# fp32 score products on both row halves, and grouped state and value products, in a gated linear attention with a feed-forward block

## The chip, the cores and the metric

The kernel runs on one core of a Trainium2 chip. The metric is the device time of one execution in microseconds; lower is better. A core has five engines with their own queues: PE (matrix products into PSUM), DVE (vectors), ACT (scalar functions), POOL (a second vector engine without access to PSUM) and SP (which issues the DMAs here). PSUM has eight banks of 512 fp32 values a row.

## The reference

Four batches, eight heads, 768 tokens, 48 channels a head. Each head keeps a 48 x 48 state that decays by alpha and takes up k times v; its rows go through a feed-forward layer of 384 -> 2048 -> 384.

```
for t in range(S):
    state = alpha[:, :, t, :, None] * state + np.einsum('bhd,bhe->bhde', k[:, :, t], v[:, :, t])
    y[:, :, t] = np.einsum('bhd,bhde->bhe', q[:, :, t], state)
...
h = x @ w_in
g = np.maximum(0.01 * h, h)
return (g @ w_out).astype(np.float32)
```

The weights come as 64-bit floats; the kernel turns each into a high and a low part of type fp32r (fp32 stored with fewer bits of mantissa, which PE takes in one pass).

## The kernel before

**Units.** The work of attention is cut into 24 units: 6 chunks of 128 tokens by 4 batches, `u = 4 * chunk + batch`. Within a chunk the products of alpha are kept as P (forward scan, L257) and 1/P (backward scan, L262), so that y = mask(scaled k times scaled q) times v, plus state times scaled q. Heads are held in pairs: head 2p in rows 0 to 47 and head 2p+1 in rows 64 to 111 of every tile, four pairs side by side. Three units make one block of 384 rows for the feed-forward part, so there are 8 blocks.

**Steps of a unit** (generator `attention`, L399): `scans`, `scores` for s = 0 and 1, `k_tokens` (k turned back by PE, L339), `scaled_q` and `scaled_k` of the unit after, `outputs` (y), `next_state` (L376, L385, L386). After every third unit `gather` moves rows of x by DMA. From unit 6 on (`SPLIT`), `parts` (L288) splits scaled k and q into high and low fp32r parts: three casts on ACT (L297, L301 twice) and three subtractions on POOL (L298, L302 twice). The two heads of a pair have columns of their own in `qh` and `ql`, zero elsewhere, so one product of 112 rows and 256 columns gives the scores of both; each pair takes three (high x high, high x low, low x high), twelve for a unit (L317), six to a PSUM bank. Each bank is then masked by one DVE product (L327). Units 0 to 5 have plain fp32 products of one head each over 48 rows (L311), and the mask of s = 0 by an ACT copy (L322) and a POOL select (L323).

**y** (`outputs`): for each of four pairs one product with the state (L354, 112 rows, both heads), then the value product of the first head (L356, into PSUM rows 0 to 47) and of the second (L357, into rows 64 to 111). ACT then casts y to its high part (L361) and DVE subtracts for the low one (L362).

**Feed-forward.** `ffn_in` (L437): nine products of 128 x 384 into bank `ph`, for each of 16 slices f; leaky maximum by ACT (L440) and DVE (L441), split by ACT (L443) and DVE (L445). `ffn_out` (L453): nine products into three banks held for the whole block. While block 0 runs, the weights are converted (L178 to L210) on ACT, DVE and POOL.

**Order.** Attention steps are called out between the feed-forward slices (L483 to L513). The framework then orders the instructions of each engine anew, by its own simulation of their times, and may keep more buffers where memory is free. PSUM: two `ph` banks, three of tag "a", three of tag "b". From unit 6 on attention uses the "b" banks in rotation for two score tiles, turned k, y and the state's product.

Of the kernel before, what the change touches and what calls it, by code (L numbers as in the profile page):

```python
# [14 lines left out]
AF = mybir.ActivationFunctionType  # L15
ALU = mybir.AluOpType

# bound on the sums of |P| and |1/P| over a chunk
RANGE = 2.0 ** 40


# [1 line left out]
def gated_linear_attn_ffn(ctx, tc, q, k, v, alpha, w_in, w_out, out):  # L23
# [34 lines left out]
    PITCH = RUN + GAP  # L58
    EARLY = 2 * UPB
    CATCH = 9  # L60
    SPLIT = EARLY
    LAG = 2
    SL = 8 * UPB

# [3 lines left out]
        return ps_x.tile([P, 512], F32, name=tag or att_bank[0])  # L68

    def pieces(name, dtype, *shapes):  # L70
        """One tile, cut into parts of these shapes a partition."""
        sizes = [math.prod(shape) for shape in shapes]
        whole = cst.tile([P, sum(sizes)], dtype, name=name)
        parts = []
        for n, shape in enumerate(shapes):
            part = whole[:, sum(sizes[:n]):sum(sizes[:n + 1])]
            axes = "abc"[:len(shape)]
            if len(shape) > 1:
                part = part.rearrange(f"p ({' '.join(axes)}) -> p {' '.join(axes)}", **dict(zip(axes, shape)))
            parts.append(part)  # L80
        return parts
# [14 lines left out]
    def load(u, i):  # L96
        if u >= NU:
            return
        tb, b = units[u]
        ts = slice(tb * C, (tb + 1) * C)  # L100
        t, src = loaded(u, i), (alpha, q, k)[i]
        if u < EARLY:
            n = H if u or i else H // 2
            for h in range(0, H, n):
                nc.sync.dma_start(
                    by_token(t)[:, h:h + n, 0:D], src[b, h:h + n, ts, :].rearrange("h t d -> t h d")
                )
            return
        # 32 partitions a head and half of its channels: runs of four tokens, shifted by 32 channels for the second
        for a in range(4):  # L110
            off = 32 * (a % 2)
            nc.sync.dma_start(
                t[32 * a:32 * (a + 1), :].rearrange("j (p r) -> j p r", p=NP)[:, :, 0:RUN - off],
                src[b, a // 2::2, ts, :].rearrange("p (j t) d -> j p (t d)", t=T4)[:, :, off:],
            )
# [29 lines left out]
        nc.gpsimd.memset(state[b], 0.0)  # L145


    # row r of group g of x is this row of w_in
    runs = [(0, D, 0, 2 * D), (D, GAP, 6 * D, GAP), (HB, D, D, 2 * D), (BR, GAP, 7 * D, GAP)]

    # the weights come as jobs: w_in and w_out for one f after the other
    jobs = {}

    def load_weights(j):
# [16 lines left out]
    def convert_1(j):  # L171
        if not f64:
            return
        raw, = jobs[j]
        words = raw.rearrange("p g (f w) -> p g f w", w=2)
        top, low = words[:, :, :, 1], words[:, :, :, 0]
        rest = cvp.tile([P, NG, P], F32, name="rest", bufs=NREST)
        nc.scalar.activation(rest, low.bitcast(U32), AF.Copy, scale=2.0 ** -52)  # L178
        # read as a float32, the upper word has the exponent in steps of eight: 2**-112 moves float64's bias to float32's
        nc.scalar.mul(top.bitcast(F32), top.bitcast(F32), 2.0 ** -112)  # L180
        jobs[j] = top, rest

# [37 lines left out]
        return bank().rearrange("r (p n) -> r p n", p=NP)  # L220

    def transposed(u, i, name, **kw):
        """The channels of a unit by rows: on TensorE into PSUM, later on VectorE into SBUF."""
        src = loaded(u, i)
        if u < EARLY:
            ps = banks4()
# [8 lines left out]
        )  # L235
        return t

    # two blocks of x; the last two heads of either come into the group between them first
    xs = {}

    live, masked = {}, {}
    q_split = [cst.tile([P, NP, 2, C], F32R, name=n) for n in ("qh", "ql")]

    # the reversed products start again from a reciprocal every STEP tokens
    STEP = 16
    nc.gpsimd.memset(seed, 0.0)

# [37 lines left out]
        nc.vector.tensor_tensor(ks, kT, rc, ALU.mult)  # L285
        live[u] = [pe, qs, ks]

    def parts(u):  # L288
        """The high and low parts of scaled k, and of scaled q with the heads of a pair in columns of their own."""
        if u == SPLIT:  # L290
            for q in q_split:
                nc.gpsimd.memset(q.bitcast(F32), 0.0)
        pe, qs, ks = live[u][:3]
        qh, ql = q_split
        kh = atp.tile([P, NP, C], F32R, name="kh", bufs=1)
        kl = atp.tile([P, NP, C], F32R, name="kl", bufs=1)
        nc.scalar.copy(kh, ks)  # L297
        nc.gpsimd.tensor_tensor(kl, ks, kh.bitcast(F32), ALU.subtract)  # L298
        for s, lo in ((0, 0), (1, HB)):
            r = slice(lo, lo + D)  # L300
            nc.scalar.copy(qh[r, :, s, :], qs[r])  # L301
            nc.gpsimd.tensor_tensor(ql[r, :, s, :], qs[r], qh[r, :, s, :].bitcast(F32), ALU.subtract)  # L302
        live[u] += [kh, kl]

    def scores(u, s):
        pe, qs, ks = live[u][:3]
        ss = banks4()
        if u < SPLIT:
            lo = s * HB
            for p in range(NP):  # L310
                nc.tensor.matmul(ss[:, p, :], ks[lo:lo + D, p, :], qs[lo:lo + D, p, :], start=True, stop=True)  # L311
        else:
            kh, kl = live[u][3:5]
            qh, ql = q_split
            for p in (2 * s, 2 * s + 1):
                for n, (kt, qt) in enumerate(((kh, qh), (kh, ql), (kl, qh))):
                    nc.tensor.matmul(  # L317
                        ss[:, 2 * (p % 2):2 * (p % 2) + 2, :], kt[0:BR, p, :], qt[0:BR, p, :, :], start=n == 0, stop=n == 2
                    )
        sm = atp.tile([P, NP, C], F32, name="sm", bufs=3)  # L320
        if u < EARLY and s == 0:
            nc.scalar.copy(sm, ss)  # L322
            nc.gpsimd.affine_select(  # L323
                out=sm, in_=sm, compare_op=ALU.is_ge, fill=0.0, base=0, pattern=[[0, NP], [1, C]], channel_multiplier=-1
            )
        else:
            nc.vector.tensor_tensor(sm, ss, mask.unsqueeze(1).broadcast_to([P, NP, C]), ALU.mult)  # L327
        masked.setdefault(u, []).append(sm)

    def masked_scores(u, p, s):  # L330
        a, b = masked[u]
        return (b if s else a)[:, p, :] if u < SPLIT else (b if p > 1 else a)[:, 2 * (p % 2) + s, :]

    def k_tokens(u):
        if units[u][0] < NC - 1:
# [8 lines left out]
    def outputs(u):  # L344
# [3 lines left out]
        V, W = vals_sb[u % NV], state[b]  # L348
        at = NG * (i % 2)
        y = banks4()  # L350
        for p in range(NP):
            r = (p + i % 2) % NP
            if tb:
                nc.tensor.matmul(y[0:BR, r, :], W[0:BR, p, :], qs[0:BR, p, :], start=True, stop=False)  # L354
            m = D if tb else HB
            nc.tensor.matmul(y[0:m, r, :], V[:, 2 * p * D:2 * p * D + m], masked_scores(u, p, 0), start=not tb, stop=True)  # L356
            nc.tensor.matmul(  # L357
                y[HB:BR, r, :], V[:, (2 * p + 1) * D:(2 * p + 2) * D], masked_scores(u, p, 1), start=not tb, stop=True
            )
        xh, xl = (x_sb[0:BR, n, at:at + NP, j * C:(j + 1) * C] for n in (0, 1))  # L360
        nc.scalar.copy(xh, y[0:BR])  # L361
        nc.vector.tensor_tensor(xl, y[0:BR], xh.bitcast(F32), ALU.subtract)  # L362
# [23 lines left out]
            nc.gpsimd.tensor_tensor(W[r, :, r], us[r], pe[r].broadcast_to([D, NP, D]), ALU.mult)  # L386

    def gather(i):
        """The last two heads go to the rows left free beside the others."""
        at = (NG + 1) * (i % 2)  # L390
        xs[i] = [x_sb[:, n, at:at + NG, :] for n in (0, 1)]
        x = x_sb.bitcast(F32)
        for g in range(NG):
            for lo in (0, HB):
                nc.sync.dma_start(x[lo + D:lo + HB, :, at + g, :], x[lo + g * GAP:lo + (g + 1) * GAP, :, NG, :])
# [1 line left out]
    ready = set()  # L397

    def attention(first, last):  # L399
        """The scaled q and k of a unit are made beside the products of the one before."""  # L400
        for u in range(first - 1, last):
            new, old = u + 1 < last, u >= first
            if new:
                scans(u + 1)
                yield
            if old:
                for s in (0, 1):
                    scores(u, s)
                    yield
                k_tokens(u)  # L410
                yield
            if new:
                scaled_q(u + 1)
                yield
                scaled_k(u + 1)
                if u + 1 >= SPLIT:
                    parts(u + 1)
                yield
            if old:
                outputs(u)  # L420
# [49 lines left out]
    while 0 not in ready:  # L470
        next(st)

    # (block, f, weight jobs and slices of attention beside it): the first block goes ahead alone, then with the second
    LEAD = NF - CATCH
    items = [(0, f, 2, SL / (CATCH - 1)) for f in range(CATCH)]
    for n in range(LEAD):
# [6 lines left out]
    for n in range(len(items) + LAG):  # L483
# [15 lines left out]
        for half in range(2):  # L499
            due += slices / 2  # L500
            while emitted < due:
                # what follows the first blocks' attention stays behind the last of the weights on VectorE
                with tc.issue_after(made[0, NF - 2].ins) if held else nullcontext():
                    next(st, None)
                held = max(held - 1, 0)
# [6 lines left out]
                    if i == 0:  # L512
                        att_bank[0], st, held = "b", attention(EARLY, NU), 5  # L513

    # the chunked form holds where no product of alphas in a chunk leaves the range; else step by step
    fine = cst.tile([P, 2 * NU], F32, name="fine")
    nc.vector.tensor_scalar(fine, acc, RANGE, None, ALU.is_lt)
    least = cst.tile([P, 1], F32, name="least")
# [8 lines left out]
    def stepwise(ctx):  # L527
        gp = ctx.enter_context(tc.tile_pool(name="gp", bufs=2))
        gps = ctx.enter_context(tc.tile_pool(name="gps", bufs=1, space=bass.MemoryType.PSUM))
        L, V = [by_token(loads_sb[i][0]) for i in range(3)], vals_sb[0]  # L530
        # the place of head h among x's rows: pieces (first e, number, row)
        place = {h: [(0, D, (h // 2) * HB)] for h in range(2 * NG)}
        for s in (0, 1):
            place[2 * NG + s] = [(g * GAP, GAP, g * HB + D) for g in range(NG)]
# [112 lines left out]
```

## Time and profile before

| | |
|---|---|
| median of 3 runs | 619.03 us (618.51 to 619.93) |
| span of the profiled execution, first to last instruction | 618.7 us |
| granted TensorE clock, mean | 0.959 |
| y products L354, L356, L357 of units 6 to 23, mean busy time of one instruction | 314, 299, 299 ns |
| feed-forward products L437, mean | 346 ns (overlapping; start to start about 173) |

A fp32 product appears as two PE instructions, a fp32r product as one. Matrix products are pipelined, so an instruction's duration is longer than the distance to the next start; the distance is the cost. "PEld" is the load of the stationary operand. A row of the timeline gives start, duration, engine, line, operation, what is written <- what is read, shape, count, and in brackets the idle time before it with what ended it.

### The profile page before, as it was taken

The page shows a single profiled execution, that of the slowest core. Times are in us where ns is not written, and L with a number is a line of the kernel's source. Part 1 is how long each engine was busy: PE and PEld are TensorE (multiplying, and loading weights), DVE is VectorE, ACT ScalarE, POOL GpSimd, SP SyncE. Part 2 cuts the span into 40 slices and gives each one's busy share as a digit, 9 for nine tenths or more (in the row PEclk, how much of TensorE's full clock was granted, in tenths as well). Part 3 has the DMA queues.
Part 4 walks back from the last instruction along what each step waited for, and adds up shares of the span by engine and source line. Part 5 has one row for each costly group of instructions (what it writes and reads, how often), then busy time and mean ns, then how long its engine had stood idle before and what let it go on. Part 6 is the DMA issues. An engine that isn't in the chain of part 4 may idle for free.

```text
span 618.7 us, 10006 instructions
## 1 busy us (share of the span) xinstructions
PE 575.9 (93%) x3634; PEld 526.4 (85%) x3634; DVE 444.9 (72%) x777; ACT 269.0 (43%) x577; POOL 205.6 (33%) x216
## 2 busy tenths in 40 slices
PE   6856998779999879999999999999999999999995
PEld 4745977779888758998898889998898989999995
DVE  5999999998999979836766678576856655333331
ACT  4656556443554425433443454243533433224332
POOL 4597588773334433400321234032220231000000
PEclk9787897989999869999999999999999999999999
DMA  9996745311533445202421244022301120011001
GB/s 167 203 190 151 179 110 149 108 51 32 149 78 77 101 105 152 58 1 55 122 48 38 55 109 110 19 65 56 100 23 37 38 70 1 1 20 40 1 1 42
DMA packets 90087, 48.11 MB, mean 78 GB/s; under 512 B 49584, under 2 KB 87984, under 8 KB 90032
## 3 DMA queue, kind: packets, MB, share of 16 engines
q1 hardware_dynamic: 90032, 47.41, 34.0%
q8 instruction: 30, 0.49, 0.3%
q14 instruction: 25, 0.20, 0.1%
HBM read 40.30 MB, written 4.72 MB: 73 GB/s over the span
## 4 chain that ended last, share of the span: by engine, by line
PE 63%; DVE 16%; issue 3%; DMA 2%; ACT 1%; SPq 1%; POOL 0%; DVEq 0%; ACTq 0%
PE a L453 25%; PE ph L437 25%; PE b L354 4%; PE b L356 3%; PE b L317 3%; DVE gl L445 2%; DVE pc L257 2%; DVE bits L199 2%; PE b L376 2%; DVE t L441 2%; DVE bits L198 2%; DVE large L210 1%; DMA small<-in_k_dram 1%; DVE pw L200 1%; DVE e L232 1%
## 5 line engine op out<-in xcount | busy, mean ns | idle before, releaser
L437 PE MATMUL ph<-large 128*128 128x384 f32 x1152 | 233.7, 346 | 7.7 <-DVE t L441 4.9
L437 PEld LDWEIGHTS ph<-large 128*128 128x128 f32 x1152 | 206.0, 193 | 13.5 <-DVE t L441 7.4
L453 PE MATMUL a<-large,gh 128*128 128x384 f32 x672 | 172.3, 343 | 0.0
L441 DVE TENSOR_TENSOR t<-ph,t 128x384 f32<-128x384 f32 x128 | 69.9, 550 | 86.2 <-ACT t L440 86.1
L453 PEld LDWEIGHTS a<-large,gh 128*128 128x128 f32 x672 | 120.2, 190 | 1.7 <-issue 0.7
L440 ACT ACTIVATE t<-ph 128x384 f32<-128x384 f32 x128 | 62.1, 489 | 117.8 <-PE ph L437 113.4
L445 DVE TENSOR_TENSOR gl<-t,gh 128x384 fp32r<-128x384 f32 x128 | 84.7, 663 | 38.1 <-ACT gh L443 37.9
L453 PE MATMUL a<-large,gl 128*128 128x384 f32 x336 | 110.5, 340 | 0.8 <-DVE gl L445 0.8
L443 ACT CAST gh<-t 128x384 fp32r<-128x384 f32 x128 | 65.4, 512 | 92.2 <-DVE t L441 91.6
L386 POOL TENSOR_TENSOR small<-us,pe 48x192 f32<-48x192 f32 x32 | 20.8, 650 | 155.1 <-DVE us L385 145.2
L453 PEld LDWEIGHTS a<-large,gl 128*128 128x128 f32 x336 | 62.8, 188 | 1.6 <-DVE gl L445 1.1
L302 POOL TENSOR_TENSOR ql<-qs,qh 48x512 fp32r<-48x512 f32 x36 | 50.0, 1388 | 8.7 <-ACT qh L301 7.3
L202 POOL TENSOR_TENSOR rest<-pw,rest 128x384 f32<-128x384 f32 x32 | 35.7, 1115 | 33.1 <-DVE pw L200 29.3
L298 POOL TENSOR_TENSOR kl<-ks,kh 128x512 fp32r<-128x512 f32 x18 | 25.2, 1400 | 60.7 <-ACT kh L297 41.0
L203 POOL TENSOR_TENSOR bits<-bits,large 128x384 f32<-128x384 f32 x32 | 38.1, 1189 | 0.7 <-ACT large L201 0.7
L268 ACT ACTIVATE e<-pc 128x512 f32<-128x512 f32 x24 | 15.2, 632 | 50.8 <-DVE rc L262 42.8
L356 PE MATMUL b<-sm,small 128*48 128x128 f32 x144 | 31.2, 299 | 3.6 <-DVE sm L327 3.6
L354 PE MATMUL b<-qs,small 112*112 112x128 f32 x144 | 33.3, 314 | 0.0
L357 PE MATMUL b<-sm,small 128*48 128x128 f32 x144 | 31.2, 299 | 0.0
L257 DVE TENSOR_TENSOR_SCAN pc<-e,small 128x128 f32<-128x128 f32 x72 | 30.1, 477 | 0.6
L354 PEld LDWEIGHTS b<-qs,small 112*112 112x112 f32 x144 | 21.1, 179 | 10.6 <-issue 10.5
L232 DVE STREAM_TRANSPOSE qs<-small 128x512 f32<-128x512 f32 x18 | 19.8, 1097 | 10.6 <-PE b L354 9.1
(93 smaller groups left out, 812.4 us busy)
## 6 DMA issues: line engine op xcount, KB each, us to landing
raw<-in_moe_w_out_dram SPq DMA_DIRECT2D x16, 384.0 KB, 3.4
small<-in_v_dram SPq DMA_DIRECT2D x24, 192.0 KB, 3.3
raw<-in_moe_w_in_dram SPq DMA_DIRECT2D x32, 144.0 KB, 3.2
out_dram<-t SPq DMA_DIRECT2D x24, 192.0 KB, 2.3
small<-in_alpha_dram SPq DMA_DIRECT2D x38, 96.0 KB, 2.2
small<-in_k_dram SPq DMA_DIRECT2D x36, 96.0 KB, 2.2
small<-in_q_dram SPq DMA_DIRECT2D x36, 96.0 KB, 2.2
small<-in_alpha_dram SPq DMA_DIRECT2D x36, 80.0 KB, 2.4
```

Of the source, the lines that this page charges most:

```text
L202: nc.gpsimd.tensor_tensor(rest, pw.bitcast(F32), rest, ALU.mult)
L203: nc.gpsimd.tensor_tensor(val, val, hi.bitcast(F32), ALU.subtract)
L257: nc.vector.tensor_tensor_scan(pc[:, p, :], aT[:, p, :], ones.broadcast_to([P, C]), 1.0, ALU.mult, ALU.mult)
L302: nc.gpsimd.tensor_tensor(ql[r, :, s, :], qs[r], qh[r, :, s, :].bitcast(F32), ALU.subtract)
L354: nc.tensor.matmul(y[0:BR, r, :], W[0:BR, p, :], qs[0:BR, p, :], start=True, stop=False)
L356: nc.tensor.matmul(y[0:m, r, :], V[:, 2 * p * D:2 * p * D + m], masked_scores(u, p, 0), start=not tb, stop=True)
L437: nc.tensor.matmul(ph, wt[:, g, fs], xt[:, g, :], start=n == 0, stop=n == 3 * NG - 1)
L440: nc.scalar.mul(t, ph, 0.01)
L441: nc.vector.tensor_tensor(t, ph, t, ALU.max)
L443: nc.scalar.copy(gh, t)
L445: made[i, f] = nc.vector.tensor_tensor(gl, t, gh.bitcast(F32), ALU.subtract)
L453: nc.tensor.matmul(po[j], gt[:, js], wt[:, f, :], start=f == 0 and n == 0, stop=f == NF - 1 and n == 2)
```

## The change

Units from 6 on lose `parts`, with its tiles `qh`, `ql`, `kh` and `kl`, and get the form of the early units: eight fp32 products of 48 rows and 128 columns, pair after pair, each pair's two heads one after the other, into two banks at once. The mask becomes a step of its own for all units: s = 0 by ACT and POOL, s = 1 by DVE. In y, the four state products come first and the eight value products behind them; only the first product of the bank has the start flag.

```
-    def parts(u):
...
-        nc.scalar.copy(kh, ks)
-        nc.gpsimd.tensor_tensor(kl, ks, kh.bitcast(F32), ALU.subtract)
...
-            nc.scalar.copy(qh[r, :, s, :], qs[r])
-            nc.gpsimd.tensor_tensor(ql[r, :, s, :], qs[r], qh[r, :, s, :].bitcast(F32), ALU.subtract)
...
+    def scores(u):
+
+        pe, qs, ks = live[u]
+        ss = [banks4(), banks4()]
+        for p in range(NP):
+            for s, lo in ((0, 0), (1, HB)):
+                nc.tensor.matmul(ss[s][:, p, :], ks[lo:lo + D, p, :], qs[lo:lo + D, p, :], start=True, stop=True)
+        live[u].append(ss)
+
+    def mask_scores(u):
+        ss = live[u].pop()
+        sm = [atp.tile([P, NP, C], F32, name="sm", bufs=3) for _ in (0, 1)]
+        nc.scalar.copy(sm[0], ss[0])
+        nc.gpsimd.affine_select(
+            out=sm[0], in_=sm[0], compare_op=ALU.is_ge, fill=0.0, base=0, pattern=[[0, NP], [1, C]], channel_multiplier=-1
+        )
+        nc.vector.tensor_tensor(sm[1], ss[1], mask.unsqueeze(1).broadcast_to([P, NP, C]), ALU.mult)
+        masked[u] = sm
...
+        if tb:
+            for p, r in enumerate(rot):
+                nc.tensor.matmul(
+                    y[0:BR, r, :], W[0:BR, p, :], qs[0:BR, p, :], start=p == 0, stop=False, skip_group_check=True
+                )
+        for p, r in enumerate(rot):
+            for s, lo, m in ((0, 0, D if tb else HB), (1, HB, D)):
+                c = (2 * p + s) * D
+                nc.tensor.matmul(
+                    y[lo:lo + m, r, :], V[:, c:c + m], masked[u][s][:, p, :],
+                    start=not tb and p == 0, stop=p == NP - 1, skip_group_check=True,
+                )
```

The order of PE's queue for y of unit 12, before (the numbers tell tiles of one name apart; `b_3231` is y, `sm_3087` and `sm_3113` the two masked score tiles, `ph` the feed-forward bank):

```order
L354 MATMUL b_3231<-qs_2912,small_73 112x128
L356 MATMUL b_3231<-sm_3087,small_73 48x128
L357 MATMUL b_3231<-sm_3087,small_73 48x128
L354 MATMUL b_3231<-qs_2912,small_73 112x128
L356 MATMUL b_3231<-sm_3087,small_73 48x128
L357 MATMUL b_3231<-sm_3087,small_73 48x128
L354 MATMUL b_3231<-qs_2912,small_73 112x128
```

The same place in the changed kernel, where L326 is the state product and L332 the value product, and `b_3142` is y:

```order
L310 MATMUL b_3069<-small_73,ks_2875 128x112 x4
L326 MATMUL b_3142<-qs_2842,small_73 112x128 x4
L332 MATMUL b_3142<-sm_3029,small_73 48x128
L332 MATMUL b_3142<-sm_3030,small_73 48x128
L332 MATMUL b_3142<-sm_3029,small_73 48x128
L332 MATMUL b_3142<-sm_3030,small_73 48x128
```

The four state products now stand together, and value products from the two masked tiles alternate behind them, eight in all. (From here on L413 is the old L437, L429 the old L453, L292 the score product, L353 the old L376, L302 the DVE mask, L339 the old L362.)

Scores on PE in the changed kernel, for unit 12 (`b_3002` is the bank of s = 0, `b_3003` that of s = 1; four more rows alternate in the same way):

```order
L429 MATMUL a_2263<-large_74,gl_2873 128x384
L292 MATMUL b_3002<-qs_2842,ks_2875 128x128
L292 MATMUL b_3003<-qs_2842,ks_2875 128x128
L292 MATMUL b_3002<-qs_2842,ks_2875 128x128
L292 MATMUL b_3003<-qs_2842,ks_2875 128x128
```

And for unit 9, with the beginning of its y (`b_2450`); before, the twelve L317 of that unit stood here in two groups of six:

```order
L292 MATMUL b_2310<-qs_2211,ks_2218 128x128 x4
L429 MATMUL a_1256<-large_74,gh_2186 128x384 x2
L429 MATMUL a_1256<-large_74,gl_2188 128x384
L429 MATMUL a_1257<-large_74,gh_2186 128x384 x2
L429 MATMUL a_1257<-large_74,gl_2188 128x384
L429 MATMUL a_1258<-large_74,gh_2186 128x384 x2
L292 MATMUL b_2311<-qs_2211,ks_2218 128x128 x4
L429 MATMUL a_1258<-large_74,gl_2188 128x384
L310 MATMUL b_2377<-small_73,ks_2218 128x112 x4
L326 MATMUL b_2450<-qs_2211,small_73 112x128 x4
L332 MATMUL b_2450<-sm_2337,small_73 48x128
L413 MATMUL ph_2264<-large_74 128x384 x3
```

In unit 12 the two halves alternate; in unit 9, as in unit 7, each half is a group of its own with feed-forward products between, and in unit 10 one group follows the other. In units 13, 16, 19 and 22 feed-forward products stand inside the scores: their eight products come in groups of 2, 5 and 1 in the first three and of 3, 2, 1, 1 and 1 in the last.

More of the change, by code (lines that the diff above doesn't have):

```diff
@@ L60, in gated_linear_attn_ffn @@
     CATCH = 9
-    SPLIT = EARLY
     LAG = 2
@@ L241, in gated_linear_attn_ffn @@
     live, masked = {}, {}
-    q_split = [cst.tile([P, NP, 2, C], F32R, name=n) for n in ("qh", "ql")]
     STEP = 16
@@ L286, in scaled_k @@
         live[u] = [pe, qs, ks]
-    def parts(u):
[L290 to L300, printed above, removed]
-            nc.scalar.copy(qh[r, :, s, :], qs[r])
-            nc.gpsimd.tensor_tensor(ql[r, :, s, :], qs[r], qh[r, :, s, :].bitcast(F32), ALU.subtract)
-        live[u] += [kh, kl]
@@ L305, in scores @@
[L305 to L328, printed above, removed]
@@ L330, in masked_scores @@
-    def masked_scores(u, p, s):
-        a, b = masked[u]
-        return (b if s else a)[:, p, :] if u < SPLIT else (b if p > 1 else a)[:, 2 * (p % 2) + s, :]
+    def scores(u):
[14 more added lines that the diff above has]
+        masked[u] = sm
@@ L350, in outputs @@
         y = banks4()
[L351 to L359, printed above, removed]
+        rot = [(p + i % 2) % NP for p in range(NP)]
+        if tb:
[10 more added lines that the diff above has]
+                )
+        del masked[u]
         xh, xl = (x_sb[0:BR, n, at:at + NP, j * C:(j + 1) * C] for n in (0, 1))
@@ L406, in attention @@
             if old:
-                for s in (0, 1):
-                    scores(u, s)
-                    yield
+                scores(u)
+                yield
+                mask_scores(u)
+                yield
                 k_tokens(u)
@@ L415, in attention @@
                 scaled_k(u + 1)
-                if u + 1 >= SPLIT:
-                    parts(u + 1)
                 yield
```

## The prediction

> **What bounds the kernel now.** I read the busy shares, then the slices, the windows, and last the timeline of single groups.
>
> ```profile
> PE 575.9 (93%) x3634; PEld 526.4 (85%) x3634; DVE 444.9 (72%) x777; ACT 269.0 (43%) x577; POOL 205.6 (33%) x216
> ...
> PE   6856998779999879999999999999999999999995
> ...
> DVE  5999999998999979836766678576856655333331
> ...
> PE 63%; DVE 16%; issue 3%; DMA 2%; ACT 1%; SPq 1%; POOL 0%; DVEq 0%; ACTq 0%
> ```
>
> Two stages. Over the first third DVE stands at 9 and PE does not; from slice 16 on PE is at 9 to the end. The windows put the border near 237 us:
>
> ```profile
> 150.00:176.80 26.80, 25.67 (x149) 24.51 (x148) 26.56 (x50) 13.85 (x31) 6.97 (x8) 1.00 0.47 117
> 176.80:200.00 23.20, 22.20 (x171) 19.17 (x170) 23.01 (x40) 8.90 (x21) 10.17 (x8) 1.00 0.38 86
> 200.00:237.00 37.00, 31.12 (x193) 25.65 (x191) 32.33 (x55) 16.73 (x38) 15.58 (x18) 0.82 0.45 104
> 203.30:206.70 3.40, 3.40 (x15) 3.30 (x16) 3.31 (x10) 0.90 (x2) 1.37 (x3) 0.50 0.87 199
> 220.40:230.60 10.20, 10.17 (x48) 7.29 (x49) 6.92 (x11) 2.03 (x5) 1.59 (x2) 0.50 0.48 110
> 250.80:545.60 294.80, 294.80 (x1900) 273.11 (x1899) 189.65 (x331) 119.04 (x251) 62.72 (x64) 1.00 0.22 52
> ```
>
> (The columns are length, busy PE, PEld, DVE, ACT, POOL, then the granted clock, DMA share and GB/s.) From 250.8 PE never rests and has its full clock, so every PE slot saved there is saved from the end. From 150 to 200 DVE is busy for 49.6 of 50 us. The changed units (numbers 6 to 23, 18 of 24) begin in that stretch. What comes before 150 us keeps its work; only its order is a little different. I cost it at nothing, because DVE has the same instructions there; the order and the buffers that the freed tiles leave room for may move it by 1.5 us either way, an estimate (about one feed-forward group). The DMAs stay the same in number and size.
>
> **The change on PE, slot by slot.** A slot is the time from one start to the next. One unit's products for y, and the feed-forward group behind them:
>
> ```profile
> 365.54 0.38 PE L354 MATMUL b<-qs,small 112*112 112x128 f32 x2
> 365.85 0.31 PE L356 MATMUL b<-sm,small 128*48 128x128 f32 x1
> 365.85 0.31 PE L357 MATMUL b<-sm,small 128*48 128x128 f32 x1
> 366.00 0.27 PE L356 MATMUL b<-sm,small 128*48 128x128 f32 x1
> ...
> 366.20 0.47 PE L354 MATMUL b<-qs,small 112*112 112x128 f32 x2
> ...
> 368.48 1.83 PE L437 MATMUL ph<-large 128*128 128x384 f32 x9
> 370.24 0.56 PE L376 MATMUL b<-small,ktok 128*48 128x48 f32 x8
> ...
> 384.72 1.72 PE L437 MATMUL ph<-large 128*128 128x384 f32 x9
> 386.28 0.52 PE L453 MATMUL a<-large,gh 128*128 128x384 f32 x2
> ```
>
> A fp32 product is two instructions. L356 and L357 start together, as they write different rows of PSUM. y takes 368.48 - 365.54 = 2.94 us. The first state product's second half comes 0.38 - 0.27 = 0.11 behind its first; later ones, behind a value product, need 0.47 - 0.27 = 0.20, and each crossing between the two shapes costs 0.20 where a slot is 0.11. Nine feed-forward products between two groups of small tiles take 1.76, and 1.56 undisturbed: 0.20 for one way in and out. Value products that follow one another show their slot earlier in the program:
>
> ```profile
> 53.43 0.27 PE L357 MATMUL a<-sm,small 128*48 128x128 f32 x1
> 53.44 0.27 PE L356 MATMUL a<-sm,small 128*64 128x128 f32 x1
> 53.54 0.27 PE L357 MATMUL a<-sm,small 128*48 128x128 f32 x1
> ```
>
> A pair every 0.11. New y: 4 state products, 8 x 0.11 = 0.87, plus 0.09 for the crossing; then 16 value instructions in 8 pairs, 0.15 + 6 x 0.11 + 0.20 = 1.00. Sum 1.96, so **0.98 us less a unit**.
>
> Scores, now and in the early units, which have the new form:
>
> ```profile
> 358.98 0.28 PE L317 MATMUL b<-qh,kh 112*128 112x256 f32 x1
> ...
> 360.42 0.26 PE L339 MATMUL b<-small,ks 112*128 112x112 f32 x1
> ...
> 29.57 1.71 PE L311 MATMUL a<-qs,ks 48*128 48x128 f32 x16
> ...
> 85.43 1.16 PE L311 MATMUL a<-qs,ks 48*128 48x128 f32 x8
> 86.52 0.32 PE L339 MATMUL a<-small,ks 112*128 112x112 f32 x1
> ```
>
> Now 12 products in 1.44 us. Four fp32 products of one half of the rows: 86.52 - 85.43 = 1.09. Eight, the halves one after the other, have 1.44 us between first and last start (1.71 - 0.27). In series that would be 15 slots of 0.11 and 0.10 more for the first, 1.78; so three slots were shared by both halves. Halves do run side by side, where the queue brings them together. With the halves alternating, I take 8 products for the time of 4: 1.09, plus 0.20 for going in and out, 1.29: **0.15 less**. Bounds: 1.09 (0.35 less) if the crossing hides, and 16 slots in series, 1.99 + 0.20 (0.75 more).
>
> [...]
>
> The order of the changed program takes some back. From unit 10 on feed-forward products break four units' scores (13, 16, 19, 22) ten extra times. A break costs the 0.20 outside and 0.19 inside a group (1.09 less 8 slots): 10 x 0.39 = 3.9. Five products lose their partner: 5 x 0.22 = 1.1. Unit 10 has its halves one after the other: 0.6. L376, the products for the next state, is broken five times where it was broken nine times: 4 x 0.39 = 1.5 back. Unit 9's rest of y gains 0.7. From unit 9's first value product on: 14 x 1.13 + 0.7 + 1.5 - 3.9 - 1.1 - 0.6 = **12.4 us less**.
>
> **The crowded stretch.** Here PE waits and its clock falls:
>
> ```profile
> 203.18 0.51 PE L317 MATMUL b<-qh,kh 112*128 112x256 f32 x1 [2.28 <-DVE large L362]
> ...
> 220.43 0.45 PE L356 MATMUL b<-sm,small 128*48 128x128 f32 x1 [3.60 <-DVE sm L327]
> ...
> 158.87 2.31 DVE L262 TENSOR_TENSOR_SCAN rc<-e,rc,small 128x511 f32<-128x511 f32 x1
> ...
> 191.53 4.50 DVE L257 TENSOR_TENSOR_SCAN pc<-e,small 128x128 f32<-128x128 f32 x4
> ...
> 216.98 2.68 DVE L257 TENSOR_TENSOR_SCAN pc<-e,small 128x128 f32<-128x128 f32 x4
> ...
> 371.38 1.37 DVE L257 TENSOR_TENSOR_SCAN pc<-e,small 128x128 f32<-128x128 f32 x4
> ...
> 191.08 1.67 POOL L298 TENSOR_TENSOR kl<-ks,kh 128x512 fp32r<-128x512 f32 x1 [2.53 <-ACT kh L297]
> 192.70 2.74 POOL L302 TENSOR_TENSOR ql<-qs,qh 48x512 fp32r<-48x512 f32 x2
> ```
>
> Unit 9's mask, late on DVE, releases PE at 220.43. DVE's four scans take 4.50 us while POOL splits k and q, and 1.37 when it does not: 3.1 us lost at once. From 157 to 219 eight DVE groups are stretched so, all beside those POOL splits, from a split at 157.88 (0.5 lost) and the scan at 158.87 to the scans at 216.98; against their clean selves they lose 8.9 us. The change takes the three POOL splits away and one of a unit's two DVE masks:
>
> ```profile
> L327 DVE TENSOR_TENSOR sm<-b,small 128x512 f32<-128x512 f32 x36 | 24.3, 682 | 3.7 <-PE b L317 3.3
> ...
> L323 POOL TENSOR_SCALAR_AFFINE_SELECT sm<-sm 128x512 f32<-128x512 f32 x6 | 4.8, 794 | 1.4 <-ACT sm L322 1.3
> ...
> L322 ACT COPY sm<-a 128x512 f32<-128x512 f32 x6 | 3.5, 581 | 1.0 <-PE a L311 0.6
> ```
>
> A DVE mask takes a slot of 0.6 there. Masks of units 6 to 8: 3 x 0.6 = 1.8 off; but unit 9's only DVE mask now stands behind a reciprocal, a copy and a backward scan, 1.7 more. So DVE gains what POOL gives back: 8.9, less what the new POOL mask takes, between nothing and 4 x 0.8. The mask ends at 211 to 215 in place of 220.3. PE gets there at about 212: its old arrival, 220.43 - 3.60 = 216.8, less the wait of 2.28 and half of the 3.4 us at half clock, less 3 x 1.13, plus 2.4 because units 7 and 9 have their halves in separate groups. Its first value products need only the POOL half, so I take 212.5, nearer to PE's end: **7.9 us less**, bounds 5 and 9.
>
> **The clock.** After the waits of 2.28 and 3.60 us come spells at half clock; the second (220.4 to 230.6, 0.50 in the window) costs 5.1 us of PE work. A wait under 2 us may leave none. I take half: **2.5 less**, bounds 0 and 5.1. [...]
>
> ACT loses three casts a unit and gains the copy; POOL loses three subtracts and gains the mask; neither bounds. In the long stage 27 feed-forward products (4.7 us) or more stand between a unit's scores and its value products; copy and mask need 0.58 + 0.79 us, and that is the cover: without it, 1.4 us a unit.
>
> Sum: 7.9 + 12.4 + 2.5 = 22.8; 618.7 - 22.8 = 595.9 of span. The runs' median stands 0.3 above the span: **596.2 us**.
>
> **Rivals.**
> - The stretch clears wholly: PE is never late and the clock holds. 0.5 more at unit 9 and 2.6 of clock: 593.1. For it: POOL falls nearly idle there. Against: DVE is full from 150 to 200 now, and loses only a mask and the stretching.
> - The stretch stays: DVE is no faster, unit 9 comes at 220.4, the spell too. Only 12.4: 606.6. For it: DVE has the same chain but one mask. Against: 4.50 beside 1.37.
> - The halves do not share slots: 0.90 a unit, on 14 units 12.6 less the 1.7 already charged, 10.9: 607.1. For it: in the 16-instruction row only three slots were shared. Against: the column pairs alternate in the same way and share every slot.
> - Slower. The halves fill two of the three PSUM banks of the attention at once, so all scores, and not the second half alone, wait for the bank of the former y, which DVE reads last (L362). At 203.18 that wait was 2.28. The gain is 22.8 / 18 = 1.27 us a unit, so it decides from 1.3 us at each unit; at 2.28 it gives 596.2 + 41.0 = 637.2. Against: in the long stage the split follows y quickly (0.8 us after y's last slot), and 18 feed-forward products stand between y and the next scores.
>
> ```profile
> 398.69 0.61 PE L453 MATMUL a<-large,gh 128*128 128x384 f32 x2
> ...
> 399.45 0.68 DVE L362 TENSOR_TENSOR large<-b,large 112x512 fp32r<-112x512 f32 x1
> ```
>
> **Chances.** Forecast 0.62 (593 to 602); wholly clear 0.12; stays 0.12; no sharing 0.08; slower 0.04; the last 0.02 unforeseen. The range takes the first three whole and reaches to the fourth: 588 to 606.8, 588 is a clear stretch with the scores' crossing hidden too (18 x 0.2 = 3.6) and 1.5 from the reordered start. By these cases faster is 0.94, slower 0.04, no change 0.02; 0.2% is about what a measurement of this kernel can tell from none.
>
> **What would show it.** y at about 2.0 us from state product to next group; scores at 1.1 where they alternate, with halves 0.01 apart; unit 9's first value product at 211 to 214; DVE's four scans back at 1.4 and POOL without subtracts; PE from 250 on still without rest. A y that stays at 2.9, scores near 2 us, or a release by the mask's copy, by POOL or by DVE's split at every unit would prove me wrong.

## The result, and the profile after

| | before | after |
|---|---|---|
| median | 619.02 us (4 runs, 618.51 to 619.93) | 596.09 us (4 runs, 594.61 to 597.35) |
| ratio | | 0.9623, 95% interval 0.9599 to 0.9646 |
| profiled execution | span 618.7 us | 594.61 us, span 592.9 us |

The profiled execution is the fastest of the four, so the two profiles lie 25.8 us apart and the medians 22.9. Of the changed kernel's lines, L299 is the POOL mask, L255 and L260 are DVE's scans, and L362 is DVE's part of the next state.

The busy shares and PE's slices after the change:

```profile
PE 550.6 (93%) x3706; PEld 516.1 (87%) x3706; DVE 414.2 (70%) x759; ACT 249.5 (42%) x541; POOL 138.7 (23%) x178
...
PE   5865989699999999999999999999999999999995
```

PE has 72 more instructions and is busy 25 us less. The windows of the stretches that the prediction used, with the same columns:

```profile
150.00:176.80 26.80, 25.34 (x157) 24.48 (x157) 25.93 (x52) 12.56 (x31) 1.15 (x4) 1.00 0.46 117
176.80:200.00 23.20, 21.17 (x178) 19.07 (x177) 22.93 (x49) 9.28 (x23) 2.99 (x7) 1.00 0.54 126
200.00:237.00 37.00, 36.18 (x272) 32.27 (x271) 35.86 (x66) 17.40 (x41) 6.24 (x10) 1.00 0.52 125
250.00:545.60 295.60, 295.31 (x2049) 279.07 (x2048) 175.17 (x322) 110.65 (x235) 21.79 (x44) 1.00 0.23 55
```

From 200 to 237 PE was busy 31.12 of 37 us at a clock of 0.82; now it is busy 36.18 at 1.00. POOL fell from 15.58 to 6.24 there. DVE is still nearly full there (35.86 of 37). From 250 on PE rests only 0.3 us. The changed groups on PE's timeline, of units 8 and 9:

```profile
196.84 1.16 PE L292 MATMUL b<-qs,ks 48*128 48x128 f32 x16
...
202.79 1.04 PE L326 MATMUL b<-qs,small 112*112 112x128 f32 x8
203.76 1.08 PE L332 MATMUL b<-sm,small 128*48 128x128 f32 x16
204.67 0.74 PE L353 MATMUL b<-small,ktok 128*48 128x48 f32 x16
...
209.43 1.16 PE L292 MATMUL b<-qs,ks 48*128 48x128 f32 x8
...
212.15 0.42 PE L332 MATMUL b<-sm,small 128*48 128x128 f32 x2
```

Sixteen score instructions with alternating halves take the same 1.16 us as the eight of one half alone (209.43): every slot is shared. y takes 204.67 - 202.79 = 1.88 us. Unit 9's first value product, at 212.15, has no wait in brackets. DVE and POOL there:

```profile
186.70 1.63 DVE L255 TENSOR_TENSOR_SCAN pc<-e,small 128x128 f32<-128x128 f32 x4
...
196.72 1.33 DVE L255 TENSOR_TENSOR_SCAN pc<-e,small 128x128 f32<-128x128 f32 x4
...
212.59 0.67 DVE L302 TENSOR_TENSOR sm<-b,small 128x512 f32<-128x512 f32 x1
...
209.70 0.81 POOL L299 TENSOR_SCALAR_AFFINE_SELECT sm<-sm 128x512 f32<-128x512 f32 x1
```

The four scans take 1.3 to 1.6 us where they took up to 4.50. Of unit 9's two masks the one on POOL is done at 210.51, before PE needs it; the one on DVE ends at 213.26, and PE runs feed-forward products until 213.77, when that unit's value products go on. All that PE still waits for between 150 and 545 us (in total, times, longest):

```profile
PE ph L413 <- DVE t L417: 2.3, 2, 1.5
PE b L292 <- DVE us L362: 0.8, 1, 0.8
PE b L292 <- DVE rc L259: 0.8, 1, 0.8
PE b L353 <- DVE t L417: 0.3, 1, 0.3
PE ph L413 <- DMA large<-large: 0.3, 1, 0.3
```

Where the 25.8 us of the two profiles lie:

| piece of the span | before | after | difference |
|---|---|---|---|
| start to unit 9's first value product | 220.43 | 212.15 | -8.3 |
| from there to unit 12's first state product | 76.65 | 69.86 | -6.8 (5.1 of it the spell at half clock) |
| from there to PE's last start | 314.84 | 303.99 | -10.9 |
| tail | 6.75 | 6.91 | +0.2 |

### The profile page after: what moved, and what is told of

The parts are those of the page before. It is cut to its first block, busy times and chain, and to the rows that moved or that the text cites. A ratio compares the mean times of both kernels' runs of the same rounds, so it can differ in the third digit from the quotient of the medians.

```text
span 592.9 us, 10070 instructions
## 1 busy us (share of the span) xinstructions
PE 550.6 (93%) x3706; PEld 516.1 (87%) x3706; DVE 414.2 (70%) x759; ACT 249.5 (42%) x541; POOL 138.7 (23%) x178
## 4 chain that ended last, share of the span: by engine, by line
PE 64%; DVE 18%; DMA 7%; SPq 3%; issue 3%; POOL 1%; ACT 1%; DVEq 0%; ACTq 0%; POOLq 0%
PE ph L413 27%; PE a L429 27%; PE b L292 3%; PE b L332 2%; PE b L326 2%; DVE gl L421 2%; DVE bits L197 2%; DMA raw<-in_moe_w_in_dram 2%; DVE large L209 2%; DVE bits L198 2%; DMA large<-large 1%; DMA raw<-in_moe_w_out_dram 1%; DVE pc L255 1%; DMA small<-in_v_dram 1%; PE b L353 1%
## 5 line engine op out<-in xcount | busy, mean ns | idle before, releaser
L413 PE MATMUL ph<-large 128*128 128x384 f32 x1152 | 232.9, 346 | 9.6 <-DVE t L417 6.7
L413 PEld LDWEIGHTS ph<-large 128*128 128x128 f32 x1152 | 206.3, 193 | 15.8 <-DVE t L417 8.7
L429 PE MATMUL a<-large,gh 128*128 128x384 f32 x672 | 174.4, 344 | 0.0
L429 PEld LDWEIGHTS a<-large,gh 128*128 128x128 f32 x672 | 119.3, 188 | 4.2 <-ACT gh L419 0.7
L429 PE MATMUL a<-large,gl 128*128 128x384 f32 x336 | 110.7, 339 | 0.0
L421 DVE TENSOR_TENSOR gl<-t,gh 128x384 fp32r<-128x384 f32 x128 | 80.8, 632 | 39.6 <-ACT gh L419 37.5
L363 POOL TENSOR_TENSOR small<-us,pe 48x192 f32<-48x192 f32 x32 | 18.3, 572 | 192.5 <-DVE us L362 191.8
L429 PEld LDWEIGHTS a<-large,gl 128*128 128x128 f32 x336 | 62.8, 188 | 0.2
L299 POOL TENSOR_SCALAR_AFFINE_SELECT sm<-sm 128x512 f32<-128x512 f32 x24 | 17.5, 731 | 90.1 <-ACT sm L298 90.1
L292 PEld LDWEIGHTS b<-qs,ks 48*128 48x128 f32 x288 | 22.5, 187 | 8.7 <-issue 6.8
L292 PE MATMUL b<-qs,ks 48*128 48x128 f32 x288 | 28.4, 289 | 1.7 <-DVE us L362 0.8
L255 DVE TENSOR_TENSOR_SCAN pc<-e,small 128x128 f32<-128x128 f32 x72 | 25.5, 414 | 0.4
L429 PE MATMUL b<-large,gh 128*128 128x384 f32 x96 | 23.3, 345 | 2.1 <-ACT gh L419 2.1
L200 ACT CAST large<-bits 128x384 fp32r<-128x384 f32 x32 | 16.3, 511 | 20.5 <-DVE bits L198 20.2
L198 DVE SCALAR_TENSOR_TENSOR bits<-raw,bits 128x384 int32<-128x384 int32 x32 | 24.8, 789 | 0.2
L227 PE MATMUL a<-small 128*128 128x128 f32 x72 | 15.6, 367 | 8.9 <-POOL small L142 3.3
```

The costliest lines, as they stand in the source:

```text
L198: nc.vector.scalar_tensor_tensor(bits, top, -0x80000000, bits, ALU.bitwise_and, ALU.bitwise_or)
L255: nc.vector.tensor_tensor_scan(pc[:, p, :], aT[:, p, :], ones.broadcast_to([P, C]), 1.0, ALU.mult, ALU.mult)
L292: nc.tensor.matmul(ss[s][:, p, :], ks[lo:lo + D, p, :], qs[lo:lo + D, p, :], start=True, stop=True)
L413: nc.tensor.matmul(ph, wt[:, g, fs], xt[:, g, :], start=n == 0, stop=n == 3 * NG - 1)
L421: made[i, f] = nc.vector.tensor_tensor(gl, t, gh.bitcast(F32), ALU.subtract)
L429: nc.tensor.matmul(po[j], gt[:, js], wt[:, f, :], start=f == 0 and n == 0, stop=f == NF - 1 and n == 2)
```

## The experiments

For each run I added up PE's slots (start to next start) by kind of instruction, from unit 12's first state product to the last start. Up to 580 us PE rests at most 0.3 us there, so the kinds add up to the time (the changed kernel's scores hold such a rest of 0.3):

| us | before | after | y alone | scores alone | halves apart | late split | alternating state | four split + alternating |
|---|---|---|---|---|---|---|---|---|
| y, 12 units | 35.50 | 23.76 | 23.50 | 35.17 | 23.75 | 23.50 | 23.75 | 23.58 |
| scores, 11 units | 15.81 | 15.41 | 16.12 | 14.44 | 19.79 | 16.11 | 15.30 | 13.74 |
| next state, 8 units | 6.86 | 6.48 | 6.22 | 7.25 | 6.47 | 6.23 | 4.59 | 4.60 |
| k turned, 7 units | 2.09 | 2.35 | 2.01 | 2.35 | 2.35 | 2.01 | 2.35 | 2.35 |
| feed-forward | 254.45 | 255.88 | 252.90 | 256.85 | 255.98 | 252.90 | 256.01 | 254.08 |
| sum, with 0.12 others | 314.84 | 303.99 | 300.88 | 316.18 | 308.46 | 300.88 | 302.13 | 298.47 |
| unit 12 begins at | 297.08 | 282.01 | 295.71 | 288.58 | 286.29 | 282.90 | 281.88 | 282.08 |
| median of the runs | 619.02 | 596.09 | 605.03 | 613.48 | 603.54 | 593.10 | 594.27 | 589.00 |

**1. y alone**, against the kernel before:

```
-        for p in range(NP):
-            r = (p + i % 2) % NP
-            if tb:
-                nc.tensor.matmul(y[0:BR, r, :], ..., start=True, stop=False)
...
+        rot = [(p + i % 2) % NP for p in range(NP)]
+        if tb:
+            for p, r in enumerate(rot):
+                nc.tensor.matmul(y[0:BR, r, :], ..., start=p == 0, stop=False, skip_group_check=True)
+        for p, r in enumerate(rot):
...
```

> The kernel before with one part of the change: y with its four state products first and its value products behind them; scores still split into high and low parts. My theory (y saves 0.98 us at each late unit, and only the score part relieves DVE and POOL): y falls from 2.94 to about 2.0 us, 14 late units give 13.7 us, the stretch at unit 9 and its clock spell stay; 603 to 606 us. Rival A (the gain is all y): 596. Rival B (the gain is all relief of DVE and POOL): 617 to 619.

605.03 us, ratio 0.9761 (0.9735 to 0.9788): as my theory had it. The wait at unit 9 stays, and three spells of 3.4 us at half clock (from 176.54, 207.26 and 231.15 on) stand where there were one of 3.4 and one of 10.2:

```profile
219.07 1.13 PE L354 MATMUL b<-qs,small 112*112 112x128 f32 x8
222.22 0.98 PE L360 MATMUL b<-sm,small 128*48 128x128 f32 x10 [2.02 <-DVE rc L261]
```

Unit 9's value products come at 222.22, later even than before (220.43), behind a wait of 2.02 us for DVE. The y of units 6 to 8 is shorter: from unit 6's first state product to unit 9's PE takes 36.6 us where it took 39.7. But PE comes to unit 6 at 182.47, 5.7 us later than before, in another order; what made this start later is not shown. The gain lies in the long stage: from unit 12 on this kernel is 314.84 - 300.88 = 14.0 us faster than before, and 3.1 us faster than the changed kernel.

**2. Scores alone**, against the changed kernel:

```
-        if tb:
-            for p, r in enumerate(rot):
...
+        for p in range(NP):
+            r = (p + i % 2) % NP
+            if tb:
+                nc.tensor.matmul(y[0:BR, r, :], ..., start=True, stop=False)
```

> The changed kernel with the other part undone: y has its state product ahead of each pair's value products again; scores are fp32 products with the halves alternating, and nothing is split. My theory: y is 2.9 us again, 0.98 more at each of 14 to 15 late units, while unit 9's first value product stays near 212 and no spell at half clock returns; 608 to 612 us. Rival A (all y): 619. Rival B (all relief): 596 to 598.

613.48 us, ratio 0.9903 (0.9878 to 0.9927). Both rivals fall and no spell returns, but the time is 1.5 us over my bound, and unit 9's first value product is not near 212:

```profile
216.01 0.39 PE L325 MATMUL b<-qs,small 112*112 112x128 f32 x2
216.32 0.42 PE L327 MATMUL b<-sm,small 128*48 128x128 f32 x2
```

It comes at 216.32 without a wait: PE itself is late, by 2.5 of these 4.2 us already at unit 6 (178.22 where the changed kernel has 175.69). Old y costs 17.4 us more than grouped y (613.48 - 596.09), and not 14 x 0.98. In the profiles it costs 12.2 us from unit 12 on and 6.6 ahead of it (288.58 against 282.01), where y alone had brought only 1.4 (295.71 against 297.08). So the parts do not add up: y alone gains 14.4, scores alone 6.0, both 23.4 on the 619.44 measured beside them. A shorter y counts ahead of unit 12 once DVE is relieved, and hardly before; how much of this is DVE's lateness and how much the other order of the early units is not separated.

**3. Halves apart**, against the changed kernel:

```
-        for p in range(NP):
-            for s, lo in ((0, 0), (1, HB)):
+        for s, lo in ((0, 0), (1, HB)):
+            for p in range(NP):
                 nc.tensor.matmul(ss[s][:, p, :], ks[lo:lo + D, p, :], qs[lo:lo + D, p, :], start=True, stop=True)
```

> The changed kernel with the order of the eight score products turned: the four of one half of the rows, then the four of the other. My theory (instructions on different row halves share a slot only where they alternate in the queue): scores of a unit take 1.8 to 2.0 us where they took 1.16 to 1.29, 0.55 to 0.9 more at each of about 13 late units, 603 to 608 us, with y and unit 9 as they are. Rival (the order in the queue does not matter, the engine finds the free half by itself): 596.

603.54 us, 0.9736 (0.9709 to 0.9764). A whole unit's scores here:

```profile
258.46 1.71 PE L292 MATMUL b<-qs,ks 48*128 48x128 f32 x16
260.10 0.62 PE L429 MATMUL a<-large,gh 128*128 128x384 f32 x2
```

260.10 - 258.46 = 1.64 us, where the changed kernel has 1.1 (255.28 to 256.38): the order in the queue decides. It is not 16 slots of 0.11, 1.76, either: some slots are still shared (in the like group at 29.57 before the change, three pairs of starts around the border between the halves lie 4 to 5 ns apart). From unit 12 on the scores take 4.4 us more, and the other kinds stay. Unit 12 begins 4.3 us later too; in this profile 1.7 of that is a spell of 3.4 us at half clock from 221.55 on, behind a wait of 2.29.

**4. Subtractions back on POOL**, against the changed kernel; their results are used nowhere:

```
+    def parts(u):
+        pe, qs, ks = live[u]
+        kl = atp.tile([P, NP, C], F32R, name="kl", bufs=1)
+        nc.gpsimd.tensor_tensor(kl, ks, ks, ALU.subtract)
+        for s, lo in ((0, 0), (1, HB)):
+            r = slice(lo, lo + D)
+            nc.gpsimd.tensor_tensor(spare[r], qs[r], qs[r], ALU.subtract)
...
+                if u + 1 >= EARLY:
+                    parts(u + 1)
```

> The changed kernel with three subtractions a unit put back on POOL (of the sizes that were removed, each of a tile from itself; the results are used nowhere). PE, ACT and DVE have the same instructions as the changed kernel. My theory (POOL's fp32 work stretches DVE's in the crowded stretch): DVE's four forward scans take 2.5 to 4.5 us there where beside idle POOL they take 1.4, unit 9's first value product comes at 216 to 220 in place of 212, and a spell at half clock may follow it; 600 to 606 us. Rival (DVE was relieved by its one mask less, not by POOL's idleness): unit 9 at 212 to 213, 596 to 597.

602.79 us, 0.9725 (0.9694 to 0.9755): 6.7 us for work on POOL that nobody waits for. All of it is lost ahead of unit 12, which begins at 290.22 in place of 282.01; from there this kernel takes 303.83 us, the changed one 303.99. Unit 9's first value product comes at 217.36. DVE runs the same 759 instructions in the same order in both kernels, PE's order differs in one pair of products, and no other engine waits for POOL between 150 and 292 us. One line of each kernel's groups (first this kernel, then the changed one) and one group of DVE and POOL of this kernel's timeline:

```profile
L255 DVE TENSOR_TENSOR_SCAN pc<-e,small 128x128 f32<-128x128 f32 x72 | 44.5, 671 | 0.4
```

```profile
L255 DVE TENSOR_TENSOR_SCAN pc<-e,small 128x128 f32<-128x128 f32 x72 | 25.5, 414 | 0.4
```

```profile
198.83 2.64 DVE L255 TENSOR_TENSOR_SCAN pc<-e,small 128x128 f32<-128x128 f32 x4
...
198.41 2.15 POOL L294 TENSOR_TENSOR ql<-qs 48x512 fp32r<-48x512 f32 x2 [2.37 <-DVE qs L275]
```

The same 72 scans cost DVE 44.5 us beside the subtractions and 25.5 without. The two subtractions of 2.15 us lay over 1.73 us of the scans and made them 1.31 longer than the changed kernel's 1.33. Then the lateness passes to PE, and to its clock (windows of this kernel):

```profile
183.70:187.10 3.40, 2.22 (x15) 1.81 (x14) 3.34 (x7) 1.24 (x3) 2.35 (x2) 1.00 0.55 132
187.10:193.90 6.80, 6.80 (x26) 6.48 (x25) 6.76 (x14) 2.81 (x8) 2.61 (x5) 0.50 0.29 71
221.20:224.60 3.40, 1.79 (x23) 1.53 (x22) 3.22 (x7) 0.58 (x2) 2.08 (x2) 1.00 0.61 145
224.60:231.40 6.80, 5.83 (x22) 5.51 (x23) 5.77 (x12) 3.33 (x8) 2.90 (x4) 0.50 0.48 115
```

PE waits 1.2 us for DVE in the first window and 2.6 us across the end of the third, where the changed kernel waits 0.8 both times, and each wait is followed by 6.8 us at half clock. Half of PE's busy time in them is 3.4 and 2.9 us: 0.4 + 1.8 + 3.4 + 2.9 = 8.5 against the 8.2 at unit 12. So in this profile most of what POOL costs is paid through the clock.

**5. Late split.** The changed kernel with scores split again from unit 12 on:

```
+    SPLITS = range(12, 24)
...
-                scores(u)
-                yield
-                mask_scores(u)
-                yield
+                if u in SPLITS:
+                    for s in (0, 1):
+                        split_scores(u, s)
+                        yield
+                else:
...
```

> The changed kernel with grouped y throughout, but scores split again into high and low parts for units 12 to 23 (casts, subtractions and both masks on DVE as before the change); units 6 to 11 keep the fp32 products. From the slots of the runs so far: from unit 12's first state product to the end the kernel with y alone takes 300.9 us, the changed one 304.0. My theory (the fp32 scores pay only in the crowded stretch, by what they take off POOL and DVE; in the long stage they cost 3.1 us, because feed-forward products break them): 3 less than the changed kernel, 592 to 594 us, with unit 9's first value product at 212 as there. Rival A (the fp32 scores pay in the long stage too): 597 to 600. Rival B (POOL's subtractions hurt there as well): 600.

593.10 us, 0.9586 (0.9564 to 0.9607), as my theory had it. From unit 12 on it takes 300.88 us, just what y alone took, and it reaches unit 12 at 282.90. In the long stage fp32 scores are the worse form: against split ones they save 0.70 us themselves (1.0 without the rest of 0.3) and cost 2.98 in the feed-forward products beside them, 0.34 in turning k, 0.25 in the next state's products and 0.26 in y. How a break looks, first in the changed kernel, then in this one (unit 13):

```profile
301.20 0.48 PE L292 MATMUL b<-qs,ks 48*128 48x128 f32 x2
301.61 0.62 PE L429 MATMUL a<-large,gh 128*128 128x384 f32 x2
```

```profile
291.81 0.34 PE L471 MATMUL a<-large,gl 128*128 128x384 f32 x1
291.98 0.28 PE L310 MATMUL b<-ql,kh 112*128 112x256 f32 x1
292.10 0.28 PE L310 MATMUL b<-qh,kl 112*128 112x256 f32 x1
```

A last fp32 product alone (two instructions) takes 0.41 where one among eight takes 1.1 / 8 = 0.14. The feed-forward products ahead of and behind such a group also have slots of 0.27 and 0.28 where others have 0.17. The first split product behind feed-forward ones takes 0.12 like the next, and the feed-forward product ahead of it 0.17: a break there costs nothing. This shows the price, not its cause inside PE.

**6 and 10. Both masks on DVE**, against the changed kernel, run twice:

```
-        nc.scalar.copy(sm[0], ss[0])
-        nc.gpsimd.affine_select(...)
+        if u < EARLY:
+            nc.scalar.copy(sm[0], ss[0])
+            nc.gpsimd.affine_select(...)
+        else:
+            nc.vector.tensor_tensor(sm[0], ss[0], mask.unsqueeze(1).broadcast_to([P, NP, C]), ALU.mult)
```

> The changed kernel with both masks of units 6 to 23 on DVE (no ACT copy and no POOL select there; the computation is the same). My theory (DVE is full from 150 to 215 and PE waits for it): each mask puts 0.6 us on DVE, three or four of them stand ahead of unit 9's y, so its first value product comes 1.8 to 2.4 us later, at 214, and a spell at half clock may follow; 597 to 602 us. Rival (POOL's idleness alone did it, DVE has room for a mask): 596.

596.50 us, 0.9636 (0.9616 to 0.9656). Unit 9's first value product came at 214.71, 2.6 later as expected, but no spell followed and the time hardly moved: my expectation missed. The changed kernel's own runs spread over 2.7 us, so both were measured again side by side.

> The changed kernel with both masks of units 6 to 23 on DVE once more, now beside the changed kernel on one chip. My theory (each mask puts 0.6 us on the full DVE; unit 9's first value product was 2.6 us later and unit 12's first state product 1.9 later in the one profile): 1.5 to 2 us slower than the changed kernel of this call. Rival (POOL's idleness alone counts): within 0.5 us of it.

596.58 us, 0.9649 (0.9634 to 0.9663), against 595.65 us, 0.9624 (0.9611 to 0.9637), for the changed kernel: 0.9 us between the medians, with intervals that overlap. That lies between the two theories; what the second mask is worth stays open, within -0.2 to 3.2 us by the ends of the intervals.

**9. The changed kernel again**, unchanged, beside run 10:

> The changed kernel once more, beside the next run on the same chip, to see how its runs spread (594.6 to 597.4 so far) and whether a spell at half clock stands between 150 and 250 us in this profile (none in the first). If half the runs have a spell, as the prediction credited half: spread of 2 to 3 us again, 595 to 598 us. If the spell is gone for good: within 1 us of 595.

594.40 to 596.75 us, median 595.65. This profile does have a spell:

```profile
218.90:222.30 3.40, 2.58 (x19) 2.26 (x19) 3.26 (x11) 1.00 (x2) 0.74 (x2) 1.00 0.72 182
222.30:225.70 3.40, 3.40 (x14) 3.30 (x13) 3.40 (x6) 2.42 (x7) 2.16 (x3) 0.50 0.60 131
```

Half clock for 3.4 us, 1.7 us of work, after 0.8 us of rest. The span is 595.0, 2.1 over the first profile. PE has the same instructions in the same order in both, so the same program runs with and without this spell.

**7. Alternating state products**, against the changed kernel:

```
-        for s, lo in ((0, 0), (1, HB)):
-            for p in range(NP):
+        for p in range(NP):
+            for s, lo in ((0, 0), (1, HB)):
                 h = 2 * p + s
```

> The changed kernel with the order of the eight products for the next state turned: the two heads of a pair one after the other, where all first heads came ahead of all second ones. They write different rows of PSUM, as the value products do. My theory (products on different PSUM rows share every slot if they stand next to each other): 16 instructions of 0.05 us take 0.4 us in place of 0.8, on 10 to 11 late units 4 us less, 591 to 593 us. Rival (48 columns are too short to gain from it, or the halves already run side by side): 596.

594.27 us, 0.9605 (0.9582 to 0.9628). The gain is real on PE and half of what I expected:

```profile
204.33 0.53 PE L353 MATMUL b<-small,ktok 128*48 128x48 f32 x16
204.79 0.44 PE L429 MATMUL a<-large,gh 128*128 128x384 f32 x1
```

0.46 us where the changed kernel's same group takes 205.34 - 204.67 = 0.67. There three of the sixteen already started 5 ns behind another, so thirteen slots became eight; my expectation had counted sixteen. From unit 12 on it is 6.48 - 4.59 = 1.9 us. The medians differ by 1.8, and the intervals overlap, so the slots carry this reading. (This profile has a spell of 3.4 us at half clock from 186.80 on.)

**8. Four units split, and alternating state products**: the edits of runs 5 and 7 with `SPLITS = (13, 16, 19, 22)`, the units whose fp32 scores are broken.

> The changed kernel with two edits: scores split into high and low parts for units 13, 16, 19 and 22 alone (there feed-forward products break the fp32 scores: 1.70 us and two extra crossings where an unbroken unit takes 1.09 and one), and the next state's products in alternating order. My theory: 0.6 to 0.8 less at each of the four units, some 3 us, and 4 us by the alternation: 588 to 591 us. If the alternation is worth nothing: 593. If splitting at four units is worth nothing: 592. Neither: 596.

589.00 us, 0.9510 (0.9489 to 0.9530): faster than both kernels, by 7 us than the changed one. From unit 12 on: 298.47, which is 3.7 under run 7 (1.6 in the scores, 1.9 in the feed-forward products, 0.2 in y).

## Why the prediction was right

The forecast was 596.2; the median is 596.09. Step by step:

- **y, 0.98 us less a unit.** Right: 35.50 - 23.76 = 11.7 over 12 units, 0.98 each.
- **Scores, 1.29 in place of 1.44, if the halves share slots.** Right: 1.09 in whole units and 0.20 in the feed-forward products on both sides of them, and run 3 shows that the alternation does it (1.64 us a unit without it, 1.1 with it). The rival without sharing was put at 0.90 a unit; run 3 gives 0.55, since a few slots are shared in series too.
- **The order takes back.** Right, and weightier than the saving. The terms for the long stage, -0.15 x 11 + 3.9 + 1.1 = 3.4, stand against 3.1 measured by runs 1 and 5 (2.8 by run 9's profile, which lacks the rest of 0.3). So the score part loses in the long stage; the prediction had the terms but never drew that sum.
- **12.4 us from unit 9's first value product on.** The profiles give 391.48 - 373.84 = 17.6, which is 12.5 and the whole spell of 5.1. That it fits to 0.1 is in part luck: by the prediction's terms 9.6 of the 12.4 fall from unit 12 on (12 x 0.98 + 11 x 0.15 - 3.9 - 1.1 + 3 x 0.39), where 10.9 were measured, and 2.8 ahead of it, where 6.8 - 5.1 = 1.7 were, as PE now rests 0.8 us there.
- **The crowded stretch, 7.9 us.** 8.3 measured, first value product at 212.15 for 212.5. That POOL's subtractions stretch DVE is shown by run 4 (four scans in 2.64 us beside two of them, in 1.33 without). PE's arrival was the bound there, as forecast: its value product at 212.15 waits for nothing, and with old y (run 2) PE comes later, again without a wait. What the mask taken off DVE gives is not settled (runs 6 and 10).
- **The clock, half of 5.1.** A size that was hedged: 5.1 came back in the first profile and 5.1 - 1.7 = 3.4 in the second. The reason given, a wait under 2 us, was not the right one: run 9's spell followed 0.8 us of rest; what the profiles show of it stands in the last section.
- **The slower rival**, scores that wait for y's split at every unit, did not come: there is no such row among the waits, only two of 0.8 us for other DVE work.

The medians moved 22.9 and the sum said 22.8; a fit this close is luck. Between the two profiles 25.8 us lie, and two terms missed in the same direction there (clock 2.6, stretch 0.4). In every run on record that lists both, the time lies 1.65 to 1.84 us above the span. By this the profile before belongs to an execution of some 620.4 us, an estimate, 1.4 above the median, while the profile after is 1.5 below its own. The 0.3 that the prediction put between span and median is therefore no fixed distance.

## What to carry to other kernels

In these runs products on different row halves, or to different rows of PSUM, shared a slot of PE only where they stood next to each other in the queue (a unit's scores 1.1 us alternating and 1.64 in halves, run 3; the next state's products 0.46 and 0.67, run 7); look at how the order breaks them before counting the sharing. A saving counts only where its engine sets the pace: ahead of unit 12 the shorter y brought 1.4 us while DVE was late, and 6.6 with POOL's subtractions gone, though the early order differed too. An engine that nobody waits for can still be the cost, through what it slows beside it: 6.7 us in run 4.

## What was not expected of the hardware

**The clock changes on a grid.** In all twelve profiles the granted clock changes only on a grid of 3.41 us; before the change, for instance, at 203.28, 206.70, 220.35 and 230.59 us, which lie 1, 4 and 3 steps apart. Cutting PE's records on that grid, from 15 us after the start on, over windows at full clock:

| PE's idle share of the window | windows | next at half clock |
|---|---|---|
| under 0.18 | 1694 | 0 |
| 0.18 to 0.30 | 63 | 1 |
| 0.30 to 0.54 | 48 | 15 |
| over 0.54 | 75 | 75 |

So in these profiles it is not one wait's length that counts (the changed kernel's longest from 150 us on, 1.5, left no spell; 0.82 us of rest in run 9 did) but how much of one window is idle: over 0.54, half clock followed in 75 of 75. Between 0.30 and 0.54 the share alone does not decide, and what else does stays open. (The ends of PE's records are modelled, so a window near a border of the table can fall on either side.) Before the change, in the two windows ahead of the spells:

```profile
199.90:203.30 3.40, 1.12 (x7) 0.80 (x6) 3.40 (x6) 2.08 (x6) 0.00 (x0) 1.00 0.32 78
216.90:220.40 3.50, 0.00 (x0) 0.00 (x0) 3.44 (x8) 1.16 (x3) 3.36 (x5) 0.99 0.53 121
```

The 2.28 us wait fell into one window (idle 0.67), and the half clock followed. The one case well under 0.30 is run 9's window at 218.90 (idle 0.24).

**POOL slows DVE's scans by more than half.** Run 4's three subtractions a unit, some 3.4 us of POOL, raise the mean scan from 414 to 671 ns. In its records all 28 scans that run beside a subtraction end 0.28 us after the end of one; the other 44 take 0.42 on average. DVE's transposes and its operations with one input in PSUM keep their times beside the same subtractions: in run 4 a transpose beside the one at 208.77 took 1.09 us and L349 (y's low part) beside the two at 211.04 took 0.69, where the changed kernel, without subtractions, has 1.08 and 0.69 (at 205.77 and 208.73). Which engine started first went with which one was slowed (run 4, POOL's subtraction alone, then one that starts behind DVE's `gl`):

```profile
195.00 1.04 POOL L291 TENSOR_TENSOR kl<-ks 128x512 fp32r<-128x512 f32 x1 [5.07 <-DVE ks L283]
...
208.67 0.56 DVE L433 TENSOR_TENSOR gl<-t,gh 128x384 fp32r<-128x384 f32 x1
...
208.77 1.36 POOL L291 TENSOR_TENSOR kl<-ks 128x512 fp32r<-128x512 f32 x1 [1.87 <-DVE ks L283]
```

Here DVE came first and kept its 0.56 us, and POOL's subtraction took 1.36 in place of 1.04. In the rows of experiment 4 POOL came first, at 198.41, and the scans from 198.83 on took 2.64 in place of 1.33. A scan that ran beside a subtraction ends 0.28 us behind it, less than the 0.42 that a scan takes alone; what lies behind this inside the engines is not shown.
